# A gated mix of linear attention and a feed-forward branch: half-word stores issued from ScalarE, fewer transposing and placing transfers, later gate products, small query instructions on GpSimd, and a new order

## The chip, the cores and the metric

The kernel runs on one core of one Trainium2 chip. The metric is the device time of one execution in microseconds (us). The profiled execution is a single one; the times are given as the median of the runs.

## The reference

For x of 2048 rows and 640 columns, 32 heads of 20 columns, and a feed-forward width of 1728, cut to what matters:

```python
qkv = (x @ wqkv).reshape(B, S, 3, H, Dh)            # H = 32, Dh = 20
pq, pk = q . w_phi, k . w_phi                       # per head, 20 x 20
phi = concat([softmax(p), softmax(-p)])             # 40 features per head
kv, z = phi_k^T v, sum_s phi_k                      # per head
o = (phi_q kv) / (phi_q z + 1e-6)
a = o @ wo                                          # branch A
b = silu(x @ w1) @ w2                               # branch B
g = sigmoid((x * gate_w).sum(-1))                   # one number per row
return g * a + (1 - g) * b
```

## The kernel before, in words

All matrix products run in fp32 with each operand split into a high and a low half and three passes (`PASSES`), so a "split" (`split`, line 228) is a copy on ScalarE and a subtraction on VectorE or GpSimd. The kernel has three stages. First the k and v projections of all rows and their features, and most of branch B. Then a tail (`TAIL`): the last tiles of branch B, the fused query weights, the split of `wo`, the query tiles t = 12 to 15, the gating of branch B's output (`out_store`, line 1267: product with 1 - g on GpSimd, then a store of the block to `fb_d` in DRAM), and the first splits of x (`xb`, line 228). Then the final stage (`FIN`): query tiles b = 0 to 11 (rows 0 to 1535), and for every pair of tiles, called a unit u, the rest of branch A. Units 0 and 1 are the tiles 12 to 15 of the tail; a unit has 256 rows.

A query tile goes: projection pq on TensorE (line 594, 30 matmuls), subtractions of maxima on VectorE, exponential on ScalarE, a product with z on GpSimd (`q_norm`, `ez`, line 1343), a sum on VectorE, small instructions on 128x32 and 128x64 (`q_parts`, `q_inv`, `q_weights`: lines 1354 to 1373), the weighting on GpSimd (`q_mul`, `eq`, line 1379), and two copies on ScalarE that write each fp32 number as two 16-bit half-words (`q_out`, lines 1389 and 1393). Two stores bring the half-words to DRAM (`m_d` and, for the last 128 columns, `t_d`). Transposing DMAs bring a unit's features back with features on partitions (`q_in`, `fT`, lines 1407 and 1411). Then pn (`n_mm`, line 1734) multiplies them with kv, and pr (`r_mm`, line 1758) the remainder that does not fill a group. The results become `oT`, split by `n_hi` and `n_lo`; those of pr are split into `rT`, stored to `r_d` (line 1771) and placed into spare partitions of `oT` by further transfers (`r_place`, line 1779). pa (`w_mm`, line 1811) multiplies oT with wo, for one or two units per oT; `w_add` adds branch B's block, loaded from `fb_d` into `y` (line 1803), and stores the result (line 1823).

`TAIL` and `FIN` are strings of names in which every name is one step. They fix the order of the instructions on TensorE, VectorE, ScalarE and GpSimd. The names used below: in `FIN`, `q{b}p`, `m`, `s`, `e`, `z`, `S`, `P`, `i`, `k`, `M`, `g` are the parts of a query tile in the order above, `j{u}{k}` transposes, `n{u}{i}` is pn, `z{u}m` is pr, `z{u}d` places, `w{p}{m}` is pa, `d{p}{m}` adds, `x..l` and `x..s` load and split a part of x. SP, which issues the DMAs, gets its order from a scheduler that follows the other engines. The DMAs share eight semaphores in turn, so an issue waits until the transfer that used its semaphore before has ended. The buffer `raw` has four slots, `oT` two.

Of the kernel before, what the change touches and what calls it, by code (L numbers as in the profile page):

```python
# [8 lines left out]
F32 = mybir.dt.float32  # L9
# [8 lines left out]
P = 128  # L18
S = 2048
D = 640  # L20
# [56 lines left out]
hm012 fm0 fs0 fl2 fl3 wa fl5 fm5 fs5 xl2 fm2 hp012 fl1 fs2 fl4 fm1 fs1 fm3 fs3 xs2 fm4 xl1 fs4 hm013  # L77
hp013 qp13 q013 wb q113 im0 km xs1 qe13 qs13 qc13 qp12 q012 qn13 q112 qe12 qN13 qP13 qs12 qc12 qn12
ia0 im1 qp14 q014 W qi13 ol1 qN12 ia1 q114 qw13 ol4 qm13 qP12 qi12 qw12 qm12 os1 hm112 qp15 q015 kp
hm113 ol0 qg13 qe14 qn14 qg12 q115 qs14 qe15 qc14 im2 qN14 ig3 qs15 hp112 qn15 ia2 qc15 qP14 qi14  # L80
ol3 qw14 qm14 hp113 im3 ia3 im4 qN15 ia4 im5 qP15 qi15 ig1 os3 ia5 im6 ia6 ig0 qw15 qm15 ol2 xl0 os2
j0 im7 qg14 ig6 ig7 os0 j1 ia7 im8 ia8 im9 j2 xs0 ig5 qg15 os4 ig8 ig9 ia9 ig2 ig4
# [61 lines left out]
TPOSE = (NP - 1,)  # L144
FIN = """
x8l q0p q0m q0s0 x3s z0m n00 n01 x6l j10 q0s1 q1p x5l z0h z0l h00 q0e q0z l00 q0S q1m q1s0 q1s1 n04
x8s x10l n10 j12 q0Z x4s n02 n11 n03 x11l h02 z1m l02 n14 j11 q0P q1e h01 n12 x7l z1h q1z n13 h10
l01 q0i x5s q2p z1l x11s q0k q1S z0d q1Z q1P h12 h11 l12 q1i q1k q0M l10 q1M x10s l11 q0g q3p q2m
q2s1 q1g z1d w00a w00b x7s q2s0 x9l q2e q2z q3m q3s1 w02a w02b q3s0 d00 q2S q3e q2Z x6s q3z q2P q2i
q2k q2M w03a q2g q3S q3Z q3P q3i q3k q3M q3g q4p q4m q4s0 q5p j20 j21 d02 j32 q4s1 q4e q4z j22 q5m  # L150
w04a z2m q5s1 w04b q5s0 z2h q5e q4S z2l n20 n21 d04 w01a q4Z q4P h20 q4i q4k q5z w01b x16l q5S x9s
q5Z q4M d01 q7p n22 n23 q4g h21 q5P l20 q7m x14l x12l n24 j30 q5i h22 z3m j31 w03b z3h n32 z3l q7s1
q5k l22 q7s0 l21 n33 x16s h31 n30 n31 h30 n34 h32 l31 l30 l32 q7e q5M q7S q6p q7z x12s z2d d03 z3d
q5g j40 w10a j42 x14s x13l q6m q6s0 q6s1 w10b w14a q7Z q7P w14b q7i q7k x13s q6e q6z q6S q8p q6Z q7M
q9p q7g z4m q6P n44 n40 q6i q6k q6M q6g q8m q8s0 d14 d10 q8s1 q8e q9m q8z n41 x17l j50 q9s0 q9s1 z4h
z4l q9e q8S x15l h40 w12a q8Z j41 w12b q8P q8i q8k h42 q9S j52 l40 q9z d12 w11a x15s w11b d11 j51
x17s q11p n42 n43 h41 q9Z q9P l42 n52 n53 q11m h51 n54 h52 q9i n50 l41 q8M q9k q9M n51 l52 z5m l51
z5h q10p w13a z5l z4d q8g h50 l50 q9g j62 q10m q10s1 q10s0 w13b z5d j61 w20a d13 q11s1 w23a w21a
w23b q10e w22a q11s0 q10S q10z w22b q10Z q11e q10P w21b w20b j60 q11S n60 n61 q10i n64 q11z q11Z h60
h62 n62 n63 q11P q11i z6m h61 z6h q10k q10M q11k q11M d22 t73 f73 t74 f74 d21 t71 f71 t72 t70 d20  # L160
t75 w24a f75 f72 w24b z7m n74 d23 l62 n72 f70 l60 n73 z6l l61 d24 z7h n70 n71 z6d w32a h70 w32b w34a
w34b z7l w30a w30b l70 h71 l71 d32 h72 l72 z7d w42a d34 w40a w42b w40b d30 d42 d40 w44a w44b d44
# [8 lines left out]
def mix_kernel(ctx: ExitStack, tc: tile.TileContext, xT, wqT, wkc, wkr, wv, bd, bdc, wo, w1, w1r, w2, out):  # L171
# [101 lines left out]
    m_d = [dp.tile([256, 2, 2 * D], U16, name=f"m_d{u}") for u in range(NP)]  # L273
    t_d = [dp.tile([256, 2, P], U16, name=f"t_d{u}") for u in range(NP)]
    r_d = [dp.tile([2, REST, 256], F32, name=f"r_d{u}") for u in range(NP)]
# [990 lines left out]
    def out_store(h, j, m):  # L1266
        nc.gpsimd.tensor_tensor(acc[j][m], acc[j][m], gates[j], op=ALU.mult)  # L1267
# [21 lines left out]
    def q_proj(t):  # L1289
# [3 lines left out]
        else:  # L1293
# [3 lines left out]
            sums[t] = pq[:, 0, HALF : HALF + 2 * H]  # L1297
# [34 lines left out]
    def q_scale(t):  # L1332

        if t // 4 == NB - 1:
            sm = Q[t]["sm"]
            nc.scalar.activation(sm[:, 6 * H :], sums[t], AF.Copy, scale=g[:, t : t + 1])
            nc.scalar.activation(sm[:, 4 * H : 5 * H], halves(sums[t])[:, :, 0], AF.Copy, scale=1e-6)
# [10 lines left out]
    def q_parts(t):  # L1348

        s, sm = sums[t], Q[t]["sm"]  # L1350
        w, parts = sm[:, 2 * H : 4 * H], halves(sm[:, 4 * H : 6 * H])
        first, other = halves(w)[:, :, 0], halves(s)[:, :, ::-1]
        if t // 4 == NB - 1:
            nc.gpsimd.tensor_tensor(first, sm[:, 4 * H : 5 * H], first, op=ALU.add)
            nc.gpsimd.tensor_tensor(parts, halves(w), other, op=ALU.mult)
        else:
            nc.vector.scalar_tensor_tensor(first, halves(s)[:, :, 0], 1e-6, first, op0=ALU.mult, op1=ALU.add)
            nc.vector.tensor_tensor(parts, halves(w), other, op=ALU.mult)
# [7 lines left out]
    def q_weights(t):  # L1366
# [3 lines left out]
        if t // 4 == NB - 1:  # L1370
            nc.gpsimd.tensor_tensor(halves(w), halves(sm[:, 6 * H :])[:, :, ::-1], rb, op=ALU.mult)
        else:
            nc.vector.scalar_tensor_tensor(  # L1373
# [562 lines left out]
```

## Time and profile before

| What | Value |
|---|---|
| median of 3 runs | 717.36 us (714.91 to 717.88) |
| the profiled execution's own time | 714.72 us |
| its span | 712.9 us |
| mean granted TensorE clock | 0.993 |
| instructions | 11989 |
| HBM traffic | 87.56 MB read, 48.02 MB written |

The profile gives each engine's busy time, the waits of an engine grouped by what ended them, the timeline of an engine (start, busy time, tile, count, and in brackets the idle time before), and windows with the granted clock. PE is TensorE's matmul part, DVE VectorE, ACT ScalarE, POOL GpSimd, SP the engine that issues DMAs here ("SPq" is its issuing). A wait is put down to what came last. The tail's query tiles start near 480 us; the final stage starts near 543 us.

### The profile page before, as it was taken

The page shows a single profiled execution, that of the slowest core. Times are in us where ns is not written, and L with a number is a line of the kernel's source. Part 1 is how long each engine was busy: PE and PEld are TensorE (multiplying, and loading weights), DVE is VectorE, ACT ScalarE, POOL GpSimd, SP SyncE. Part 2 cuts the span into 40 slices and gives each one's busy share as a digit, 9 for nine tenths or more (in the row PEclk, how much of TensorE's full clock was granted, in tenths as well). Part 3 has the DMA queues.
Part 4 walks back from the last instruction along what each step waited for, and adds up shares of the span by engine and source line. Part 5 has one row for each costly group of instructions (what it writes and reads, how often), then busy time and mean ns, then how long its engine had stood idle before and what let it go on. Part 6 is the DMA issues. An engine that isn't in the chain of part 4 may idle for free.

```text
span 712.9 us, 11989 instructions
## 1 busy us (share of the span) xinstructions
PE 692.9 (97%) x4492; PEld 585.5 (82%) x4492; DVE 469.4 (66%) x774; ACT 310.1 (43%) x544; POOL 389.2 (55%) x296
## 2 busy tenths in 40 slices
PE   8999999999999999999999999999999789899997
PEld 7888888888888888888888888778987668688877
DVE  4587988886343556678525656666886869868832
ACT  5444454546555243235344324435383344633330
POOL 2367876585743465132875547801579776646320
PEclk9999999999999999999999999999999999999999
DMA  8458878676775557185966633473077776788753
GB/s 305 139 180 300 320 269 319 241 279 229 228 250 168 186 207 243 52 294 199 302 223 228 216 109 114 171 216 99 19 196 235 199 201 191 229 191 196 213 158 100
DMA packets 98968, 146.46 MB, mean 205 GB/s; under 512 B 47779, under 2 KB 63159, under 8 KB 98911
## 3 DMA queue, kind: packets, MB, share of 16 engines
q1 hardware_dynamic: 98910, 145.71, 63.6%
q8 instruction: 35, 0.57, 0.3%
q14 instruction: 23, 0.18, 0.1%
HBM read 87.56 MB, written 48.02 MB: 190 GB/s over the span
## 4 chain that ended last, share of the span: by engine, by line
PE 82%; DMA 7%; DVE 3%; POOL 2%; SPq 2%; ACT 2%; issue 2%; POOLq 0%; DVEq 0%
PE kvp L618 17%; PE o L1234 11%; PE a L1104 9%; PE pa L1811 8%; PE o L1193 8%; PE pq L594 5%; PE b L1104 3%; PE c L1104 3%; PE d L1104 3%; PE o_m L1256 3%; DMA oT<-r_d 2%; PE ph L684 2%; PE hp L703 2%; PE kvt L605 1%; DMA out<-y 1%
## 5 line engine op out<-in xcount | busy, mean ns | idle before, releaser
L1224 DVE TENSOR_TENSOR acc<-acc,o 128x512 f32<-128x512 f32 x104 | 68.4, 683 | 35.3 <-PE o L1234 35.2
L618 PE MATMUL kvp<-wh,xa 128*128 128x480 f32 (+2 forms) x420 | 90.3, 358 | 0.0
L1811 PE MATMUL pa<-oT,wo 128*128 128x512 f32 (+1 forms) x375 | 75.0, 359 | 6.8 <-DMA oT<-r_d 4.2
L1193 PE MATMUL o<-u,w 128*128 128x512 f32 x340 | 81.2, 390 | 0.1
L618 PEld LDWEIGHTS kvp<-wh,xa 128*128 128x128 f32 x420 | 72.8, 188 | 9.9
L1811 PEld LDWEIGHTS pa<-oT,wo 128*128 128x128 f32 x375 | 61.3, 194 | 18.8 <-issue 8.6
L1193 PEld LDWEIGHTS o<-u,w 128*128 128x128 f32 x340 | 63.5, 188 | 14.0 <-DVE u L677 0.5
L1343 POOL TENSOR_TENSOR ez<-eq,zbc 128x1280 f32<-128x1280 f32 x16 | 47.2, 2953 | 27.6 <-ACT eq L1326 25.9
L594 PE MATMUL pq<-wq,xb 128*128 128x320 f32 x360 | 55.2, 311 | 1.4 <-POOL xb L228 1.4
L594 PEld LDWEIGHTS pq<-wq,xb 128*128 128x128 f32 x360 | 53.1, 188 | 4.1 <-issue 1.8
L1120 POOL TENSOR_TENSOR u<-v,u 128x512 fp32r<-128x512 f32 x16 | 20.7, 1292 | 64.2 <-ACT u L1119 64.2
L1118 ACT ACTIVATE v<-v 128x512 f32<-128x512 f32 x33 | 20.9, 632 | 78.8 <-DVE v L1137 36.5
L646 POOL TENSOR_TENSOR ek<-ek,st 128x1280 f32<-128x1280 f32 x16 | 38.3, 2394 | 30.9 <-DVE st L645 25.7
L1088 POOL TENSOR_TENSOR v<-v,v 128x512 f32<-128x512 f32 x32 | 41.6, 1302 | 13.7 <-DVE u L1120 7.0
L618 PE MATMUL kvp<-wl,xa 128*128 128x480 f32 (+2 forms) x210 | 47.6, 356 | 0.0
L1379 POOL TENSOR_TENSOR eq<-eq,sm 128x1280 f32<-128x1280 f32 x16 | 38.3, 2397 | 14.2 <-DVE sm L1373 13.8
L1389 ACT COPY ez<-eq 128x2400 uint16<-128x2400 uint16 x14 | 30.7, 2194 | 31.3 <-POOL eq L1379 31.3
L228 POOL TENSOR_TENSOR xb<-xrb,xb 128x512 fp32r<-128x512 f32 (+1 forms) x18 | 19.6, 1098 | 41.8 <-PE pwq L346 26.1
L228 POOL TENSOR_TENSOR xa<-xra,xa 128x512 fp32r<-128x512 f32 (+1 forms) x26 | 28.4, 1112 | 23.8 <-ACT xa L226 17.6
L618 PEld LDWEIGHTS kvp<-wl,xa 128*128 128x128 f32 x210 | 36.6, 188 | 4.8
L1120 DVE TENSOR_TENSOR u<-v,u 128x512 fp32r<-128x512 f32 x25 | 19.9, 797 | 29.5 <-ACT u L1119 28.1
L1267 POOL TENSOR_TENSOR acc<-acc,G 128x512 f32<-128x512 f32 x20 | 28.7, 1458 | 13.7 <-DVE acc L1198 13.7
(251 smaller groups left out, 1542.2 us busy)
## 6 DMA issues: line engine op xcount, KB each, us to landing
w<-w_d SPq DMA_DIRECT2D x20, 640.0 KB
w_d<-aw SPq DMA_DIRECT2D x14, 640.0 KB
m_d<-ez SPq DMA_DIRECT2D x14, 640.0 KB
sa<-s_d SPq DMA_DIRECT2D x16, 512.0 KB
xr<-xT SPq DMA_DIRECT2D x27, 256.0 KB
ra<-w SPq DMA_DIRECT2D x18, 320.0 KB
wb<-w_d SPq DMA_DIRECT2D x9, 640.0 KB
w_k<-w SPq DMA_DIRECT2D x8, 640.0 KB
```

The costliest lines, as they stand in the source:

```text
L228: eng.tensor_tensor(lo, src, hi.bitcast(F32), op=ALU.subtract)
L594: nc.tensor.matmul(dst, xt[c][:, hx, :], w[:, c, hw, lo : lo + n], start=first, stop=(hx == 1 and c == NC - 1))
L618: nc.tensor.matmul(kv_cols(t, lo, hi), xt[c][:, hx, :], WKV[hw][:, c, w_cols(lo, hi)], start=(n == 0), stop=(n == 3 * NC - 1), skip_group_ ...
L646: return lambda: nc.gpsimd.tensor_tensor(groups(e), groups(e), spread(st[:, 1, :]), op=ALU.mult)
L1088: nc.gpsimd.tensor_tensor(v[i], v[a], v[b], op=ALU.subtract)
L1104: last["mm"] = nc.tensor.matmul(out, lhs, rhs, start=(first and i == 0), stop=(stop and i == len(todo) - 1), skip_group_check=True)
L1120: eng.tensor_tensor(u[:, 1, :], v, u[:, 0, :].bitcast(F32), op=ALU.subtract)
L1193: nc.tensor.matmul(o, lhs, rhs, start=(n == 0), stop=(n == len(todo) - 1))
L1224: nc.vector.tensor_tensor(acc[j][m], acc[j][m], o, op=ALU.add)
L1234: nc.tensor.matmul(o, ws[hw], x()[hx], start=(first and i == 0), stop=(i == len(PASSES) - 1), skip_group_check=True)
L1343: nc.gpsimd.tensor_tensor(ez, Q[t]["e"], zbc, op=ALU.mult)
L1811: nc.tensor.matmul(pa[:, a, :], wo_tile[0][:, c, hw, ds], o[:, ho, c, :size], start=(i == 0), stop=(i == len(TERMS) - 1),)
```

## The change

Five edits, and with them new strings for `TAIL` and `FIN`.

1. In `q_out` the two stores of half-words are issued by ScalarE, not SP. The 128 last columns go into `m_d` beside the others, so `t_d` is gone, and `q_in` needs three transposing DMAs for a unit, not four.
2. `r_d` and `oT` are laid out so that `r_place` needs two transfers for a unit, not four.
3. The small steps `q_parts` and `q_weights` of the twelve tiles of `FIN` run on GpSimd (three instructions) with two scalings on ScalarE (`q_scale`), as those of tiles 12 to 15 already do, not on VectorE.
4. The low half of the split of `wo` (five times 128x640) is computed on GpSimd.
5. The gate products of block 2 of branch B (rows 1024 to 1535) leave the tail: they are done in `FIN` on the loaded block `y` (`w_gate`, names `c{p}{m}`), with a load of the gates of its own (`late_gates`, name `gl`) into one of the four raw slots.

```diff
 TAIL = """
-hm012 fm0 fs0 fl2 fl3 wa fl5 fm5 fs5 xl2 fm2 hp012 fl1 fs2 fl4 fm1 fs1 fm3 fs3 xs2 fm4 xl1 fs4 hm013
+hm012 hp012 ol2 fl5 ol3 fl4 fm0 ol4 xl1 fl2 fl3 fm5 fs5 fm4 fm3 fl1 fm1 fs0 fm2 fs4 fs3 km fs2 xs1
...
 FIN = """
-x8l q0p q0m q0s0 x3s z0m n00 n01 x6l j10 q0s1 q1p x5l z0h z0l h00 q0e q0z l00 q0S q1m q1s0 q1s1 n04
+q0p j12 x4s x5l q1p z0m n00 q0m q0s1 q0s0 q1m q0e q0z n01 q1s0 q1s1 x3s x5s n02 q1e j11 x6l q0S q0c
...
     def out_store(h, j, m):
-        nc.gpsimd.tensor_tensor(acc[j][m], acc[j][m], gates[j], op=ALU.mult)
         b = 2 * h + j
+        if b != NB - 2:
+            nc.gpsimd.tensor_tensor(acc[j][m], acc[j][m], gates[j], op=ALU.mult)
...
-        split(wo_tile[0][:, c, 0], wo_tile[0][:, c, 1], r[:, :D])
+        split(wo_tile[0][:, c, 0], wo_tile[0][:, c, 1], r[:, :D], "pool")
...
     def q_scale(t):
 
-        if t // 4 == NB - 1:
-            sm = Q[t]["sm"]
-            nc.scalar.activation(sm[:, 6 * H :], sums[t], AF.Copy, scale=g[:, t : t + 1])
-            nc.scalar.activation(sm[:, 4 * H : 5 * H], halves(sums[t])[:, :, 0], AF.Copy, scale=1e-6)
+        sm = Q[t]["sm"]
+        nc.scalar.activation(sm[:, 6 * H :], sums[t], AF.Copy, scale=g[:, t : t + 1])
+        nc.scalar.activation(sm[:, 4 * H : 5 * H], halves(sums[t])[:, :, 0], AF.Copy, scale=1e-6)
...
-            nc.vector.scalar_tensor_tensor(first, halves(s)[:, :, 0], 1e-6, first, op0=ALU.mult, op1=ALU.add)
-            nc.vector.tensor_tensor(parts, halves(w), other, op=ALU.mult)
+        nc.gpsimd.tensor_tensor(first, sm[:, 4 * H : 5 * H], first, op=ALU.add)
+        nc.gpsimd.tensor_tensor(parts, halves(w), other, op=ALU.mult)
...
+        nc.gpsimd.tensor_tensor(halves(w), halves(sm[:, 6 * H :])[:, :, ::-1], rb, op=ALU.mult)
...
-        nc.sync.dma_start(m_d[u][rows], main)
-        nc.sync.dma_start(t_d[u][rows], rest)
+        nc.scalar.dma_start(m_d[u][rows, :, : 2 * D], main)
+        nc.scalar.dma_start(m_d[u][rows, :, 2 * D :], rest)
...
-        n = min(4, 2 * NG - 4 * k)
+        n = min(4, 2 * NG + 1 - 4 * k)
...
         if n < 4:
-            nc.sync.dma_start_transpose(d[:, n], t_d[u].rearrange("t s c -> (t s) c"))
-            fTs[u, NG] = f[:, n * 256 : (n + 1) * 256]
+            fTs[u, NG] = f[:, (n - 1) * 256 : n * 256]
...
     def r_place(u):
         for side in range(2):
             rows = slice(side * CT + KD, (side + 1) * CT)
-            for s in range(2):
-                nc.sync.dma_start(
-                    o_cols(u)[rows, s].bitcast(F32),
-                    r_d[u][s, side * REST // 2 : (side + 1) * REST // 2].rearrange("(c r) s -> r c s", r=CT - KD),
-                )
+            nc.sync.dma_start(
+                o_cols(u)[rows].rearrange("r c s w -> r (c s) w").bitcast(F32),
+                r_d[u][side * REST // 2 : (side + 1) * REST // 2].rearrange("(r c) s w -> r (c s) w", r=CT - KD),
+            )
...
+    def w_gate(p, m0):
+        y = ws[p, m0][0]
+        n, size, at = w_parts(p, m0)
+        at -= (NB - 2) * 512
+        g = gates["late"][:, None, at : at + size].to_broadcast([P, n, size])
+        nc.gpsimd.tensor_tensor(y, y, g, op=ALU.mult)
```

The order moves at three places that matter below. On TensorE, where the tail meets the final stage, before (pq_5481 is the second query tile of `FIN`, q1, pq_5592 the third, q2; two more pq follow it, and then the first pa):

```order
L594 MATMUL pq_5481<-wq,xb_4_4893 128x320
L1734 MATMUL pn_2_5533<-fT_2_5393,kvw 64x256 x2
L1734 MATMUL pn_0_5541<-fT_0_5478,kvw 64x256 x2
L1758 MATMUL pr_5561<-fT_2_5544,kvwr 64x128 x2
L1734 MATMUL pn_2_5565<-fT_2_5544,kvw 64x256 x2
L1734 MATMUL pn_1_5574<-fT_1_5568,kvw 64x256 x4
L594 MATMUL pq_5592<-wq,xb_0_5465 128x320 x2
```

And now, with pq_5521 for q2 and pq_5626 for q3:

```order
L1730 MATMUL pn_0_5488<-fT_0_5395,kvw 64x256 x4
L595 MATMUL pq_5521<-wq,xb_0_5504 128x320 x2
L1730 MATMUL pn_1_5566<-fT_1_5514,kvw 64x256 x4
L1763 MATMUL pr_5574<-fT_2_5444,kvwr 64x128 x2
L1730 MATMUL pn_2_5577<-fT_2_5303,kvw 64x256 x2
L1730 MATMUL pn_0_5621<-fT_0_5619,kvw 64x256 x2
L595 MATMUL pq_5626<-wq,xb_0_5504 128x320 x2
```

Unit 1's pr and most of its pn now come behind q2's projection; behind them q3, q4 and q5 stand ahead of the first pa, where q2 and q3 stood. On GpSimd the end of the tail and the start of `FIN`, before:

```order
L1379 TENSOR_TENSOR eq_5189<-eq_5189,sm_5187 128x1280
L1267 TENSOR_TENSOR acc_3_2400<-acc_3_2400,G_2_5113 128x512
L228 TENSOR_TENSOR xb_0_5396<-xrb_0_5337,xb_0_5396 128x512
L1267 TENSOR_TENSOR acc_1_2406<-acc_1_2406,G_3_5115 128x512
L228 TENSOR_TENSOR xb_0_5465<-xrb_0_5422,xb_0_5465 128x512
L1343 TENSOR_TENSOR ez_5525<-eq_5461,zbc 128x1280
L228 TENSOR_TENSOR xb_4_5536<-xrb_4_5426,xb_4_5536 128x256
```

And now:

```order
L1370 TENSOR_TENSOR eq_5208<-eq_5208,sm_5206 128x1280
L1270 TENSOR_TENSOR acc_1_2398<-acc_1_2398,G_3_4983 128x512
L230 TENSOR_TENSOR xb_2_5446<-xrb_2_5408,xb_2_5446 128x512
L1343 TENSOR_TENSOR ez_5498<-eq_5443,zbc 128x1280
L230 TENSOR_TENSOR xb_0_5504<-xrb_0_5406,xb_0_5504 128x512
L230 TENSOR_TENSOR xb_4_5507<-xrb_4_5449,xb_4_5507 128x256
L1353 TENSOR_TENSOR sm_5441<-sm_5441 128x32
```

The products with G_2 are gone, both xb splits of the second pair of tiles stand behind the products with G_3, one of them behind the first tile's ez, and the small instructions follow. On SP around the placing transfers of unit 1 (into oT_5522), before:

```order
L1779 DMA oT_5522<-r_d_119 4x5x256 x2
L1394 DMA m_d_104<-ez_5525 128x2560
L1395 DMA t_d_112<-sm_5459 128x256
L321 DMA xrb_2_5945<-xT 128x2x256
L1394 DMA m_d_104<-ez_5581 128x2560
L1407 DMA_TRANSPOSE fT_0_5862<-m_d_104 128x4x512
```

And now (into oT_5560):

```order
L1783 DMA oT_5560<-r_d_110 4x10x256 x2
L322 DMA xrb_2_5684<-xT 128x2x256
L1783 DMA oT_5560<-r_d_111 4x10x256
L1398 DMA_TRANSPOSE fT_0_5734<-m_d_104 128x4x512
L1783 DMA oT_5560<-r_d_111 4x10x256
L1398 DMA_TRANSPOSE fT_1_5829<-m_d_104 128x4x512
L1398 DMA_TRANSPOSE fT_2_5856<-m_d_104 128x3x512
```

The stores are no longer in SP's row. Between the two placing transfers of unit 1 stands the first transpose of unit 2 (m_d_104).

More of the change, by code (lines that the diff above doesn't have):

```diff
@@ L272, in mix_kernel @@
     g_d = dp.tile([NT, P], F32, name="g_d")
-    m_d = [dp.tile([256, 2, 2 * D], U16, name=f"m_d{u}") for u in range(NP)]
-    t_d = [dp.tile([256, 2, P], U16, name=f"t_d{u}") for u in range(NP)]
-    r_d = [dp.tile([2, REST, 256], F32, name=f"r_d{u}") for u in range(NP)]
+    m_d = [dp.tile([256, 2, 2 * D + P], U16, name=f"m_d{u}") for u in range(NP)]
+    r_d = [dp.tile([REST, 2, 256], F32, name=f"r_d{u}") for u in range(NP)]
     X = {}
@@ L1707, in mix_kernel @@
             ):
+                if part is q_out and PB.index(t // 2) in TPOSE:
+                    continue
                 ops[f"{name}{t}"] = lambda t=t, part=part: part(t)
-        for k in range(3):
+        for k in range(0 if 0 in TPOSE else 3):
             ops[f"j{k}"] = lambda k=k: q_in(0, k)
@@ L1849, in mix_kernel @@
                 ops[f"d{p}{m0}"] = lambda p=p, m0=m0: w_add(p, m0)
+                if p > 2:
+                    ops[f"c{p}{m0}"] = lambda p=p, m0=m0: w_gate(p, m0)
+        ops["gl"] = late_gates
         for b, t in enumerate(QT):
```

92 lines of the change are left out of this document (51 added, 41 removed).

## The prediction

> **What bounds the kernel now.** I read the page first, then the list of waits, TensorE's timeline after 540 us, its clock by windows, and SP's and POOL's timelines around each wait. The page:
>
> ```profile
> PE 692.9 (97%) x4492; PEld 585.5 (82%) x4492; DVE 469.4 (66%) x774; ACT 310.1 (43%) x544; POOL 389.2 (55%) x296
> ```
>
> TensorE is busy 97% of the span, and the order of the two kernels shows the same matmuls in both. So only time in which TensorE waits or runs slowly can be won. All its waits after 480 us, as total, times, longest:
>
> ```profile
> PE pa L1811 <- DMA oT<-r_d: 4.2, 4, 3.4
> PE pr L1758 <- DMA fT<-t_d: 3.8, 1, 3.8
> PE pa L1811 <- DMA out<-y: 2.7, 1, 2.7
> PE pq L594 <- POOL xb L228: 1.4, 1, 1.4
> PE pwq L346 <- DMA wTq<-wqT: 1.2, 1, 1.2
> PE pn L1734 <- DVE sm L1363: 0.7, 1, 0.7
> ```
>
> They add up to 14.0 us. The timeline shows that more is lost behind three of them (start, busy time, count, wait in brackets):
>
> ```profile
> 546.03 3.19 PE L594 MATMUL pq<-wq,xb 128*128 128x320 f32 x20 [1.40 <-POOL xb L228]
> ...
> 561.12 0.69 PE L1758 MATMUL pr<-fT,kvwr 128*64 128x128 f32 x4 [3.76 <-DMA fT<-t_d]
> 561.57 2.80 PE L1734 MATMUL pn<-fT,kvw 120*64 120x256 f32 x12
> 564.30 9.28 PE L594 MATMUL pq<-wq,xb 128*128 128x320 f32 x60
> 577.02 10.54 PE L1811 MATMUL pa<-oT,wo 128*128 128x512 f32 x38 [3.44 <-DMA oT<-r_d]
> ...
> 622.56 8.67 PE L1811 MATMUL pa<-oT,wo 128*128 128x512 f32 x30 [2.65 <-DMA out<-y]
> ...
> 641.62 7.16 PE L1811 MATMUL pa<-oT,wo 128*128 128x512 f32 x30
> ...
> 654.93 2.38 PE L1734 MATMUL pn<-fT,kvw 120*64 120x256 f32 x20 [0.75 <-DVE sm L1363]
> ```
>
> The undisturbed price of 30 pa is 7.16 us, and the same 30 took 8.67 behind the wait of 2.65: 1.51 too many. 38 pa should take 38/30 x 7.16 = 9.07 and took 10.54: 1.47. Twelve pn should take 12/20 x 2.38 = 1.43 and took 2.80: 1.37. The windows say why; the last number but two of each row is the granted clock:
>
> ```profile
> 561.00:564.30 3.30, 3.18 (x16) 1.80 (x16) 2.50 (x5) 1.06 (x3) 2.17 (x2) 0.50 0.77 176
> 577.00:587.50 10.50, 10.48 (x39) 8.33 (x40) 5.00 (x9) 1.75 (x3) 7.42 (x5) 0.84 0.91 241
> 622.50:631.20 8.70, 8.64 (x31) 7.01 (x32) 7.28 (x14) 2.36 (x2) 6.24 (x4) 0.81 0.91 218
> 641.60:648.70 7.10, 7.10 (x33) 5.82 (x32) 6.93 (x12) 2.84 (x5) 6.85 (x4) 1.00 0.92 230
> ```
>
> Each of the three waits is followed by a stretch at a lowered clock, which costs about 1.45 us more (4.35 in all); the wait of 1.40 us is not (20 pq in 3.19 us is the rate of the 60 in 9.28). The pool to win from is 14.0 + 4.35 = 18.4 us. The Trainium skill ("TensorE: Matmul & The Clock Gate", section "Part 1: The HAM clock gate") says that the clock falls to half after about 3.4 us of idleness and needs 3.4 us of work to come back; the 0.50 behind 3.76 us agrees, while 2.65 us, which by it should have cost nothing, did lower the clock here. By the page the third stretch could not be won back by shortening its wait, and the sum below would be 1.5 us worse.
>
> **What ends these waits.** SP issues all transfers in one row, so what stands ahead there delays what TensorE needs (issue time, then the tile):
>
> ```profile
> 558.23 1.25 SPq L1411 DMA_TRANSPOSE fT<-t_d  x1
> ...
> 570.09 0.59 SPq L1779 DMA_DIRECT2D oT<-r_d  x2
> 572.70 0.37 SPq L1394 DMA_DIRECT2D m_d<-ez  x1
> ...
> 573.59 1.27 SPq L1779 DMA_DIRECT2D oT<-r_d  x2
> ```
>
> The fourth transpose of unit 1 leaves at 558.23, and pr of that unit waits for it until 561.12. The last two placing transfers stood behind a store that had to wait for ScalarE's copies: all of SP's waits of this kind, and the landing (from the chain) of the transfer that pa waits for:
>
> ```profile
> SPq L1394 <- ACT sm L1393: 13.4, 7, 3.8
> 573.59 3.30 DMA oT<-r_d
> 609.63 5.52 DMA out<-y
> 616.83 2.97 SPq L1779 DMA_DIRECT2D oT<-r_d  x8
> ```
>
> At the second oT the output store of 609.63 was under way for 5.52 us; SP's next issue after the stores behind it stood until 615.1, and the eight placing transfers left from 616.83 on.
>
> **The change part by part.**
>
> Stores on ScalarE. 28 issues leave SP, and with them SP's 13.4 us of waiting for the copies. ScalarE waits only for its own copies, so no wait for them is new; but an issue can stand until the transfer that had its semaphore before has ended. Bounds for 28 issues: 0.37 us each (row at 572.70), 10 us of an engine that is busy 43%, so nothing on the path; at worst a block of 3.8 us (the longest above) once or twice, behind which stand the splits of xb and the oT copies. I take 0.5 us on the path.
>
> Fewer transfers. The fourth transpose (1.25 us of SP) goes in seven units, and the remainder comes with the last transpose. Placing takes 2 instead of 4 per unit; each costs about 0.3 to 0.37 us (0.59 for 2, 2.97 for 8), 16 fewer is 5 to 6 us of SP over 150 us. These bring forward by 1.2 and 0.6 us what stands behind; alone that shortens the waits of 3.76 and 3.44 by as much.
>
> The order of TensorE. A whole pair of query tiles' worth of work moves: pq2 now stands ahead of pr and most of pn of unit 1, pq4 and pq5 stand ahead of the first pa, pq8 and pq9 ahead of the second oT's pa. One pq is 30 matmuls, half of 9.28: 4.6 us. So pr of unit 1 has 4.6 us more cover, plus 1.2, against a wait of 3.76; the first pa 9.3 more against 3.44; the second oT's pa 9.3 more against 2.65. If transfers kept their times, all three would vanish, with their slow stretches.
>
> They don't keep them: the cover moves the next unit's stores and transposes too. In SP's new order the last placing transfer of unit 1 stands behind the first transpose of unit 2, which waits for unit 2's stores. I follow that unit through POOL with the rows of the next part, in the times of before. xb for pq2 is complete at 555.7 (worked out there); then come a split of 0.73, an ez of 2.95, two mul of 2.40, the small ops of two tiles (1.8) and ScalarE's copies, for which 2.6 is taken (mul's length and a little): 568.6. POOL's waits for its partners are 3.0 us a tile now (24.1 + 13.9 less 1.7, over 12), so one to two tiles' waits make it 571.6 to 574.6; I take 573.1. The store lands some 1.5 later, the transpose takes 1.25 to issue as at 558.23, and the placing transfer behind it 0.6 and 3.30 as above: 579.8. pa stood at 577.0; without the earlier waits and their slow stretch (1.4 + 0.6 + 3.76 + 1.37 + 3.44 = 10.6), with two pq more ahead (8.9, the two in 9.28 less their modelled end) and the new waits below (2.0 + 0.3) it is due at 577.6. So 2.2 us of wait and one slow stretch of 1.45 stay (between 0.7 with none and 5.2 with it, for the 1.5 us either way). The pa of the second oT comes out even (its transfers land 0.2 us before it is due): 0 to 5, I take 1.0.
>
> POOL. Its rows (all after 540 us, by form; busy, mean | idle before):
>
> ```profile
> L1343 POOL TENSOR_TENSOR ez<-eq,zbc 128x1280 f32<-128x1280 f32 x12 | 35.3, 2948 | 24.1 <-ACT eq L1326 22.4 <-DMA m_d<-ez 1.7
> L1379 POOL TENSOR_TENSOR eq<-eq,sm 128x1280 f32<-128x1280 f32 x13 | 31.2, 2403 | 13.9 <-DVE sm L1373 13.8
> L228 POOL TENSOR_TENSOR xb<-xrb,xb 128x512 fp32r<-128x512 f32 x11 | 14.1, 1280 | 6.6 <-ACT xb L226 6.6
> L228 POOL TENSOR_TENSOR xb<-xrb,xb 128x256 fp32r<-128x256 f32 x5 | 3.6, 728 | 4.2 <-ACT xb L226 4.2
> L1267 POOL TENSOR_TENSOR acc<-acc,G 128x512 f32<-128x512 f32 x7 | 9.4, 1370 | 0.0
> L1357 DVE SCALAR_TENSOR_TENSOR sm<-pq,sm 128x32 f32<-128x32 f32 x12 | 2.3, 190 | 0.3
> L1358 DVE TENSOR_TENSOR sm<-sm,pq 128x64 f32<-128x64 f32 x12 | 2.6, 221 | 0.4
> L1373 DVE SCALAR_TENSOR_TENSOR sm<-pq,g,sm 128x64 f32<-128x64 f32 x12 | 3.2, 274 | 0.2
> L1354 POOL TENSOR_TENSOR sm<-sm x4: 253/254/256, 509.1 to 534.6; 128x32 f32<-128x32 f32 x4
> L1355 POOL TENSOR_TENSOR sm<-sm x4: 320/323/325, 509.4 to 535.0; 128x64 f32<-128x64 f32 x4
> L1371 POOL TENSOR_TENSOR sm<-sm x4: 305/500/972, 513.2 to 538.4; 128x64 f32<-128x64 f32 x4
> L1336 ACT ACTIVATE sm<-sm,g x4: 329/348/350, 503.1 to 527.0; 128x64 f32<-128x64 f32 x4
> ```
>
> The small instructions cost VectorE 190 + 221 + 274 = 0.69 us a tile, and POOL 0.254 + 0.323 + 0.305 to 0.97 = 0.88 to 1.55 us (from the four tiles that already go that way), with 0.35 and a smaller one on ScalarE. A pair of tiles holds POOL now for 2 x (2.95 + 2.40) + 2 x 1.28 + 0.73 = 14.0 us, then for 15.8 to 17.1. TensorE needs for a pair 9.28 (pq) + 2.38 (pn) + 1.25 x 7.16 (37.5 pa) = 20.6. So POOL stays under TensorE, and the handshakes sit in its idle time; but the path from pq to the store grows by 0.2 to 0.9 us a tile, which I have counted above. VectorE's 8.2 us were beside matmuls already: nothing. Here a rule speaks against the change: the Trainium skill ("GPSIMD Engine Reference", section "4.1 Engine selection") puts elementwise work on VectorE and calls GpSimd about twice as slow with two inputs; 323 against 221 ns is 1.5. By twice, a pair would hold POOL for 16.7 us.
>
> The split of wo goes to POOL five times; 128x640 lies between the 1.28 for 512 and 1.28 + 0.73 for 768 columns: 1.6 us each, 8.0 in all, against five gate products taken away, 6.9. Ahead of the tail's last mul stand the 8.0 more and three products (4.1) less:
>
> ```profile
> 539.41 2.83 POOL L1379 TENSOR_TENSOR eq<-eq,sm 128x1280 f32<-128x1280 f32 x1
> ```
>
> It ended at 542.2 and now ends up to 3.9 us later; since POOL is 55% busy, most of the five splits fall into idle time, and I take 1.1: 543.3. Then come five products (6.85), a split of xb (1.28), an ez that stood behind it before (2.95), and the other split (1.28): xb for pq2 is complete at 555.7. TensorE, rid of the first two waits but for 0.6, begins pq2's products with the low halves at about 554.2 (from 546.03: less 1.4 and 0.6, then 3.1 left of pq0, 4.6 for pq1, 1.0 for pr and six pn, 1.5 for ten matmuls). That is a new wait of 1.5 us, 2.0 with half a microsecond for POOL's hand-overs on the way; the bounds are 0.4 and 4.8 (mul later by 0 or 3.9), and with a slow stretch 6. It is shorter than the waits after which the clock fell, so I add no slow stretch.
>
> The late gate products: six on POOL, four of 1.37 and two of about 0.73, 6.9 us, of which a third stands behind the last tile, where POOL is free. They stand ahead of the last additions, which come after the matmuls; cover is there, price 0 to 0.7, I take 0. The gates' load holds one of four raw buffers, so some xb load starts later: 0 to 1.4 (the xb wait above), I take 0.3. ScalarE's two further table loads lie in the tail beside matmuls: 0.
>
> **Sum.** What stays or comes: first weight wait halved 0.6, pq2 2.0, pq4 0.3 (a split between two ez), raw buffer 0.3, first pa 2.2 + 1.45, second pa 1.0, ScalarE's issues 0.5, the small waits at the end (4.2 less 3.4 at the last oT, and a little of DVE's 0.7) 0.9 = 9.3. 18.4 - 9.3 = 9.1 us less. The profiled execution took 714.7, below the median of 717.4 and just under the lowest of the three runs; on it the sum is 705.6, on the median 708.3, which I take.
>
> **Rivals.** (1) All waits go, as the cover of 4.6 to 9.3 us alone would say: 16 to 18.4 less, 699 to 701. For it: every covered wait is under 4 us. Against: the placing behind the transpose in SP's row.
> (2) The waits only move: pq2 waits 5 to 6 us for xb with a slow stretch, the first pa keeps 5.2, the second pa gets 3 plus 1.45: about 17 against 18.4, 715 to 718. For it: POOL and SP have each got a new thing ahead of what TensorE needs.
> (3) The new issuer does not do what it says. The Trainium skill ("DMA: Bandwidth & Descriptors", section "Issuing engines are not separate DMA queues") holds that issuing from a further engine saves only the sequencer's time, usually little. As a mechanism of this kernel: the transfers land no earlier, since the engines share the load that the window at 577 shows (0.91 busy). Then 3.3 us of landing becomes 5.5 as in the output store's row, the first pa keeps another 2.2 and the second too: 4.4 less gain, about 713. Against: the wait at 573.59 was for SP's turn, not for bandwidth.
> (4) Slower: GpSimd becomes the bound of the query pairs. It holds 15.8 to 17.1 us by itself; its idle time for the partner engines is now (22.4 + 13.8)/12 = 3.0 a tile, 6.0 a pair. If that doesn't shrink, and three small ops more wait for partners, a pair takes 21.8 to 23.1 against 20.6. Six pairs at 2.0 to 2.5 are 12 to 15 us lost against 9.1 won: 720 to 724. It decides from 1.5 us a pair. Against: that idle time is mostly because POOL runs ahead.
>
> **Chances.** The forecast 0.46, with its own range 704 to 713; (1) 0.13; (3) 0.10; (2) 0.19; (4) 0.12. Faster or slower by 0.5% (about what a measurement of this kernel can tell from none) means below 713.8 or above 720.9. Faster: the forecast, (1), most of (3) and a little of (2), 0.67; same: the rest of (3), most of (2), a little of (4), 0.21; slower 0.12. The range of 699 to 719 leaves out (4) and the outermost parts of (1) and (2), under 2 in 10.
>
> **What would show it.** No wait of pr for a transposing transfer, and the 12 pn behind it at full clock; a wait of pq for xb of 1 to 4 us near 556; the first pa waiting 1 to 4 us for oT; no wait over 1.5 us at the second oT; POOL under 17.5 us busy per pair. I am wrong if POOL's ez or mul stands at the end of TensorE's waits pair after pair, if ScalarE's issues block for several us ahead of xb or oT copies, or if the transposes land later than 4 us after their issue.

## The result, and the profile after

The changed kernel is slower: 723.94 us median (722.44 to 726.0) against 716.63 of the kernel before in the same comparison, a ratio of 1.011 with a 95% interval of 1.006 to 1.015. In a second comparison it was 1.011 again (1.007 to 1.015). The profiled execution has a span of 722.2 us, 9.3 more than before. First its page, then all that TensorE waited for after 470 us (total, times, longest):

```profile
PE 694.9 (96%) x4492; PEld 586.9 (81%) x4492; DVE 455.1 (63%) x733; ACT 317.9 (44%) x570; POOL 405.2 (56%) x338
```

```profile
PE pa L1815 <- DMA out<-y: 5.6, 1, 5.6
PE pn L1730 <- DVE oT L1755: 4.5, 2, 3.2
PE pa L1815 <- DMA y<-fb_d: 3.5, 1, 3.5
PE pa L1815 <- DMA xrb<-xT: 3.3, 1, 3.3
PE pa L1815 <- DMA oT<-r_d: 2.0, 2, 1.3
PE pn L1730 <- DMA fT<-m_d: 1.5, 2, 0.9
PE pq L595 <- POOL xb L230: 1.4, 1, 1.4
PE pr L1763 <- DMA fT<-m_d: 0.2, 1, 0.2
```

These are 22.0 us, where the same list gave 14.0 before. pr's wait of 3.8 has shrunk to 0.2, as forecast, and the weights' 1.2 is gone, of which the forecast had left half. In their place stand waits of pa at every oT, 14.4 us in five places, and of pn, for VectorE above all. TensorE's timeline shows where they are and the slow work behind three of them:

```profile
554.40 3.30 PE L595 MATMUL pq<-wq,xb 128*128 128x320 f32 x20 [1.44 <-POOL xb L230]
...
565.52 0.65 PE L1730 MATMUL pn<-fT,kvw 120*64 120x256 f32 x4 [3.24 <-DVE oT L1755]
566.11 6.20 PE L595 MATMUL pq<-wq,xb 128*128 128x320 f32 x30
572.24 0.65 PE L1730 MATMUL pn<-fT,kvw 120*64 120x256 f32 x4
572.82 9.06 PE L595 MATMUL pq<-wq,xb 128*128 128x320 f32 x60
585.22 8.71 PE L1815 MATMUL pa<-oT,wo 128*128 128x512 f32 x30 [3.34 <-DMA xrb<-xT]
...
632.70 7.47 PE L1815 MATMUL pa<-oT,wo 128*128 128x512 f32 x31 [3.49 <-DMA y<-fb_d]
...
671.45 17.67 PE L1815 MATMUL pa<-oT,wo 128*128 128x512 f32 x68 [5.63 <-DMA out<-y]
```

30 pq took 6.20 us where half of 9.06 is due (1.7 too many), 30 pa took 8.71 for 7.16 (1.55), and 68 pa took 17.67 for 16.23 (1.4): 4.6 us, about the 4.35 of before. So 8.0 us more of waits and 0.3 more of slow work stand against the 9.3 that the span has grown. By the two pages the 9.3 are 7.3 us of idle time and 2.0 of busy time; of the busy time the slow stretches account for 0.3, and the rest isn't traced here. In a wait for transfers the profile names whatever landed last; SP's timeline tells more. Around the first pa of the changed kernel:

```profile
577.88 0.62 SPq L1783 DMA_DIRECT2D oT<-r_d  x1
578.60 2.18 SPq L1398 DMA_TRANSPOSE fT<-m_d  x1
580.84 0.63 SPq L1783 DMA_DIRECT2D oT<-r_d  x1
```

The last placing transfer does stand behind the transpose, as forecast. But SP had stood still for 7.9 us ahead of the first of these two, and not for a store:

```profile
SPq L1783 <- DVE oT L1755: 7.9, 1, 7.9
```

The placing writes rows of oT that `n_lo` also writes, so it waits for all of the unit's low halves. These are late for two reasons. One of unit 1's products stands on TensorE behind the projection of 566.11, which itself came late and ran slow; it starts at 572.24 (above), and its copy on ScalarE ends at 573.5. And on VectorE five instructions of the next tiles, from 572.34 on, stand ahead of the two halves, which start at 576.80: about 3.3 us of the wait are VectorE's fixed order. Besides, each issue itself costs more than it did. The issues of the store to r_d and of the placing, before and then changed (minimum, median, maximum in ns):

```profile
L1771 SPq DMA_DIRECT2D r_d<-rT x16: 274/344/496, 559.6 to 690.1; - x16
L1779 SPq DMA_DIRECT2D oT<-r_d x32: 242/295/851, 562.5 to 697.3; - x32
```

```profile
L1776 SPq DMA_DIRECT2D r_d<-rT x16: 752/790/1091, 562.7 to 700.9; - x16
L1783 SPq DMA_DIRECT2D oT<-r_d x16: 612/653/1345, 567.5 to 703.9; - x16
L1385 ACTq DMA_DIRECT2D m_d<-ez x14: 541/542/644, 521.2 to 665.2; - x14
L1386 ACTq DMA_DIRECT2D m_d<-sm x14: 541/580/825, 521.9 to 665.9; - x14
```

Half as many placing transfers take the same time in all (32 x 0.295 = 9.4 us, 16 x 0.653 = 10.4), and the store to r_d, of which there are as many as before, takes 16 x 0.446 = 7.1 us more.

### The profile page after: what moved, and what is told of

It is laid out like the page before. It is cut to its first block, busy times and chain, and to the rows that moved or that the text cites. A ratio compares the mean times of both kernels' runs of the same rounds, so it can differ in the third digit from the quotient of the medians.

```text
span 722.2 us, 11976 instructions
## 1 busy us (share of the span) xinstructions
PE 694.9 (96%) x4492; PEld 586.9 (81%) x4492; DVE 455.1 (63%) x733; ACT 317.9 (44%) x570; POOL 405.2 (56%) x338
## 4 chain that ended last, share of the span: by engine, by line
PE 87%; DMA 5%; DVE 3%; SPq 2%; issue 1%; POOL 0%; ACT 0%; ACTq 0%; POOLq 0%
PE kvp L619 17%; PE o L1194 11%; PE o L1235 11%; PE a L1105 9%; PE pa L1815 8%; PE pq L595 6%; PE ph L685 3%; PE b L1105 3%; PE c L1105 3%; PE d L1105 3%; PE o_m L1257 3%; DMA out<-y 2%; PE hp L704 2%; DMA oT<-r_d 2%; PE kvt L606 1%
## 5 line engine op out<-in xcount | busy, mean ns | idle before, releaser
L230 POOL TENSOR_TENSOR xb<-xrb,xb 128x512 fp32r<-128x512 f32 (+1 forms) x18 | 19.8, 1106 | 26.6 <-ACT xb L228 25.9
L1105 PE MATMUL a<-xo,wc 128*128 128x512 f32 x132 | 33.5, 389 | 0.0
```

The source lines that it names most:

```text
L230: eng.tensor_tensor(lo, src, hi.bitcast(F32), op=ALU.subtract)
L1105: last["mm"] = nc.tensor.matmul(out, lhs, rhs, start=(first and i == 0), stop=(stop and i == len(todo) - 1), skip_group_check=True)
```

## Experiments

All ratios are to the kernel before, timed on the same chip in the same comparison. In two kernels, `order_alone` and `small_on_vector`, the VectorE form of the small steps reads the sums after the reciprocal has been written over them, so that their output isn't the reference's. The number, shape and order of their instructions are those meant, and their times are used for that alone.

**The order and the edits, apart.** First all edits in the old order; then the new order without the edits.

> All five edits of the change, but with the order of TAIL and FIN before; only the steps that did not exist before are added to it (the scalings right behind a tile's sum, the late gates' load behind unit 1's first copy of pn's result, each late product ahead of its addition). Theory 1 (the new order puts transposes and long waits ahead of the placing transfers): the edits alone win what they save on SP, 710 to 716 us, and TensorE's waits for pn behind VectorE are absent. Theory 2 (the edits themselves, above all small instructions on GpSimd and the placing that waits for the whole unit, cost the time): 720 us or more, with pn or pa waiting as in the changed kernel.

> The new order of TAIL and FIN with none of the other edits: stores on SP, four transposes and four placing transfers for a unit, the small query instructions on VectorE (on sums kept in SBUF, as the new order needs the PSUM bank free), the split of wo on VectorE, the gate products of block 2 in the tail. Theory 1 (the order is at fault): 722 us or more, since SP then has more to issue in the same places. Theory 2 (the edits are at fault): 708 to 714 us.

```diff
# parts_in_old_order: strings of before, with the new names put in
-... q0e q0z l00 q0S q1m ...
+... q0e q0z l00 q0S q0c q1m ...
# order_alone, in the changed kernel: each edit taken back
-        nc.scalar.dma_start(m_d[u][rows, :, : 2 * D], main)
+        nc.sync.dma_start(m_d[u][rows], main)
```

Measured: 734.08 us, 1.028 (1.026 to 1.031), and 728.29 us, 1.021 (1.018 to 1.023). The first is in the range of theory 2, the second in that of theory 1, so neither theory alone holds: each half alone is slower than the two together. The order needs the edits, the edits need the order, and the cost has to be looked for piece by piece.

**Two edits taken back in the changed kernel.**

> The changed kernel with the three small query instructions of the twelve late tiles back on VectorE, reading sums in SBUF; no scalings on ScalarE for them. Theory A (VectorE stands still in its fixed row for small results that are queued behind GpSimd's long products, and so releases the banks of pn late): the two waits of pn for VectorE (3.2 and 1.3 us) and the slow 1.6 us behind the first go, and the transposed units come earlier: 714 to 719 us. Rival (VectorE is late by its own work and the order): the waits stay within 1 us of these and the time within 721 to 726.

> The changed kernel with the stores of half-words issued by SP again (three transposes for a unit and the joint buffer stay). Theory A (ScalarE's issues that wait for a semaphore of another transfer hold up the oT copies): TensorE's wait of 3.5 us at the second oT goes, 717 to 721 us. Rival (SP is the crowded row, and taking the stores off it helped): 726 to 732 us, with longer waits of pa.

```diff
# small_on_vector, in q_parts and q_weights
-        nc.gpsimd.tensor_tensor(parts, halves(w), other, op=ALU.mult)
+        nc.vector.tensor_tensor(parts, halves(w), other, op=ALU.mult)
# stores_on_sp, in q_out
-        nc.scalar.dma_start(m_d[u][rows, :, 2 * D :], rest)
+        nc.sync.dma_start(m_d[u][rows, :, 2 * D :], rest)
```

Measured: the small instructions on VectorE 728.2 us, 1.019 (1.015 to 1.022). They do not help in the new order; against the changed kernel's 1.011 they cost some 5 us there. Theory A falls, and the time is above the rival's range too. The stores on SP 722.2 us, 1.011 (1.009 to 1.014): who issues the stores makes no difference to the time. pn's long wait for VectorE went, the first pa's wait grew to 7.5 us, and neither expectation was met.

**The other edits, taken back one at a time.**

> The changed kernel itself, beside the others on one chip. Both theories: 1.007 to 1.015 of the kernel before, 719 to 726 us, with a first pa that waits 3 to 4 us and slow pa behind it.

> The changed kernel with the placing of before: r_d and oT in their old layouts, four placing transfers for a unit. In the changed kernel's trace an issue of the r_d store takes 0.79 us on SP where it took 0.34 before, and one of the two placing transfers 0.65 where one of the four took 0.30: the merged layout saves no issue time and costs 16 x 0.45 = 7 us of SP. Theory D (SP's time decides when the second and third oT are whole): issue times fall back to 0.34 and 0.30, the waits of pa (3.5 and 5.6 us) shrink by 2 us or more, 717 to 721 us. Rival (SP has room, and the order decides): within 1.5 us of the changed kernel's time on this chip.

> The changed kernel with the joint buffer undone: the last 128 half-word columns go to a buffer of their own, and a unit takes four transposes. Stores took 0.54 + 0.58 us to issue in the changed kernel, 0.36 + 0.39 before. Theory D: the stores' issues fall back to these times, SP issues seven more transposes of about 1.2 us; if SP is what counts, 724 to 730 us and longer waits of pn and pr for transposes. Rival (the joint buffer's slower stores are what hurts): 717 to 721 us.

> The changed kernel with the gate products of block 2 back in the tail and no late load. Theory (the raw slot and the late products cost nothing): xb for the third tile is 4 to 7 us later, since five more products stand ahead of it on GpSimd, and pq waits that long: 724 to 730 us. Rival (the raw slot held to the end delays loads of x and with them the first pa, which the trace names as waiting for an xb load): 717 to 721 us.

```diff
# old_placing: r_d, oT, the store in r_lo and r_place as before
-        oTs[p] = tb.tile([P, NG, 2, 512], F32R, tag="oT", name=f"oT{p}", bufs=2)
+        oTs[p] = tb.tile([P, 2, NG, 512], F32R, tag="oT", name=f"oT{p}", bufs=2)
# four_transposes
+        nc.sync.dma_start_transpose(d[:, n], t_d[u].rearrange("t s c -> (t s) c"))
# gates_early, in out_store
-        if b != NB - 2:
+        if True:
```

Measured: the changed kernel 721.02 us, 1.011 (1.007 to 1.015); with the old placing 714.45 us, 1.0005 (0.998 to 1.003); with four transposes 721.21 us, 1.012 (1.008 to 1.016); with early gates 725.76 us, 1.017 (1.014 to 1.020). The old placing came out below both of its ranges. So the placing with its new layouts is what the change lost, about 1% or 7 us. The late gates gain some 5 us, as their theory had it, and the joint buffer is even. TensorE's waits with the old placing (four longest groups):

```profile
PE pn L1730 <- DVE oT L1755: 4.5, 2, 3.2
PE pa L1816 <- DMA oT<-r_d: 2.6, 1, 2.6
PE pa L1816 <- DVE sm L1360: 2.5, 1, 2.5
PE pa L1816 <- DVE eq L586: 2.3, 1, 2.3
```

The two waits at the last two oT are gone and the others of pa are shorter; pn's are not. At the end of the kernel the chain from rT to oT of the last two units can be read off SP's timeline; with the old placing, and then the changed kernel in the same comparison:

```profile
682.92 0.69 SPq L1776 DMA_DIRECT2D r_d<-rT  x2
686.51 1.30 SPq L1784 DMA_DIRECT2D oT<-r_d  x4
...
690.23 0.67 SPq L1776 DMA_DIRECT2D r_d<-rT  x2
693.17 1.28 SPq L1784 DMA_DIRECT2D oT<-r_d  x4
```

```profile
687.17 1.68 SPq L1776 DMA_DIRECT2D r_d<-rT  x2
691.86 1.36 SPq L1783 DMA_DIRECT2D oT<-r_d  x2
...
697.23 1.65 SPq L1776 DMA_DIRECT2D r_d<-rT  x2
700.35 1.36 SPq L1783 DMA_DIRECT2D oT<-r_d  x2
```

From the store's issue to the end of the placing's issues it is 4.9 and 4.2 us with the old placing, and 6.1 and 4.5 with the new: the two stores of a unit alone take 1.0 us longer to issue.

**The store or the placing.**

> The changed kernel with half of its placing undone: r_d and oT keep the new layout (so the store from rT to r_d, 0.79 us to issue), but a unit is placed by four transfers, not two. Theory D1 (the store's new form is the slow part: from its issue to the placing 4.7 us at the end of the kernel, where the old placing took 2.9): 718 to 722 us, pa still waits at the two last oT. Theory D2 (the merged placing transfers, which wait for all of a unit's halves and land later, are the slow part): 713 to 717 us.

> The changed kernel with the other half undone: r_d in its old layout with the old store (0.34 us to issue), but a unit is placed by two transfers. Theory D1: 713 to 717 us. Theory D2: 718 to 722 us.

> The kernel before, its order and all its steps, with only the new layouts of r_d and oT and two placing transfers for a unit. Theory D (the placing chain of every unit is 2.4 us longer, from the end of rT to pa): each of the four waits of pa for oT grows by up to 2.4 us, 717 to 724 us, 3 to 10 more than before. Rival (it costs only where the new order has no slack): within 2 us of before.

```diff
# merged_store_only, in r_place
+            for s in range(2):
+                nc.sync.dma_start(o_cols(u)[rows, :, s].bitcast(F32), ...)
# merged_placing_only, in r_lo
-                r_d[u][:, :, k * P : (k + 1) * P], t[k * CT : k * CT + REST].bitcast(F32)
+                r_d[u][:, :, k * P : (k + 1) * P].rearrange("s r c -> r s c"), t[k * CT : ...]
```

Measured: 724.59 us, 1.014 (1.010 to 1.017); 716.34 us, 1.003 (1.000 to 1.005); 717.74 us, 1.005 (1.002 to 1.007). Theory D1 fits better, though the first time lies above its range: with the store back in its old form, two placing transfers are nearly as good as four. The issues in the kernel with the merged placing only, then in that with the merged store only:

```profile
L1776 SPq DMA_DIRECT2D r_d<-rT x16: 289/336/660, 563.4 to 692.6; - x16
L1783 SPq DMA_DIRECT2D oT<-r_d x16: 609/630/761, 566.5 to 695.5; - x16
```

```profile
L1776 SPq DMA_DIRECT2D r_d<-rT x16: 752/788/1109, 562.2 to 697.6; - x16
L1784 SPq DMA_DIRECT2D oT<-r_d x32: 611/616/828, 566.6 to 701.9; - x32
```

The last row is a flaw of that experiment: four transfers out of the new layout cost 0.62 each, not 0.30, so it charges the store with some 9 us of SP that are the placing's. It also shows what made a placing transfer dear. In the new layout one of four costs 0.62 and one of two 0.65, so merging does halve the issue time there; but the new layout doubles the price of each. The comparison of the changed kernel with the merged placing only is clean of the flaw, and gives 1.011 against 1.003 (each in its own comparison). SP's order at the end of the kernel is the same in these two, while with the old placing the last unit's store goes ahead of a load of `y`; with the merged placing only, the chains of the last two units take 4.9 and 3.9 us against the 6.1 and 4.5 above. The issues of the store differ between these two as 0.79 and 0.34 us; whether the store also lands later was not separated from that. In the old order the new placing costs 0.5%, at the lower edge of theory D's range.

**What the order left.** With the old placing the new order is even with before, not 9 us faster. SP had the cause in its waits: 8.9 us in one piece for VectorE's halves.

> The changed kernel with the old placing, and in FIN a few steps moved: on VectorE the low half that frees a bank of pn (l02) goes ahead of the wait for GpSimd's small result, the two low halves of unit 1 ahead of the next tile's subtractions and the sum, one low half of unit 3 ahead of a sum; and the first transposes of the next unit behind the placing of units 1 and 3. TensorE's order is the same. Theory E (SP's placing stood for up to 8.9 us for halves that were late in VectorE's fixed row, and for transposes; the bank was late for the same reason): the waits of 3.2 (pn), 2.6 and 2.5 us (pa) shrink to under 1 each, with slow stretches 8 to 10 us less than with the old placing alone: 704 to 709 us. Rival (what is moved back makes new waits: the later subtractions and transposes): 712 to 717 us.

> The version with the old placing and the halves moved ahead, and besides unit 1's third transpose ahead of a load of x and of the late gates on SP. In the version without that, pn waited 3.1 us for this transpose (issued at 561.7 behind the two loads, 1.8 us) and the next tile's projection ran slow behind it. Theory E: the wait shrinks by 1.5 to 2 us and the slow stretch shortens, 707 to 710 us. Rival (the load of x that comes later holds the next projection): 711 to 714 us.

> The changed kernel, its own placing included (new layouts, store of 0.79 us, two placing transfers), with only the steps of FIN moved as in the version with the halves ahead. Theory D (the store's form lengthens the chain of every unit from rT to pa by 2.4 us; where there is slack it costs nothing): 714 to 718 us, the first pa no longer waits over 1 us, the last two oT still cost 1 to 1.5 us each. Rival (the loss was the halves' place in the order alone): 710 to 713 us.

```diff
# steps of FIN, in the changed kernel's string (excerpts)
-... x8s q1i q1k q1M j10 n10 h02 q2s1 q3p l11 q2s0 n11 l02 ...
+... x8s h02 l02 q1i q1k q1M j10 n10 q2s1 q3p l11 q2s0 n11 ...
-... q3m q0g q3s1 x6s q2e q3s0 ... h10 q2z x9s q2S l10 l12 q2c q4p j20 ...
+... q3m q0g x6s q2e ... h10 q2z x9s l10 l12 q3s1 q3s0 q2S q2c q4p ... z1d j20 ...
# transpose_earlier, besides
-... n02 q1e j11 x6l ... z1h gl x9l ... j10 n10 ...
+... n02 q1e j11 j10 x6l ... z1h x9l ... h02 gl l02 ...
```

Measured: 711.75 us, 0.995 (0.993 to 0.998); 708.37 us, 0.991 (0.988 to 0.994); with the changed kernel's own placing 721.52 us, 1.008 (1.005 to 1.010). The first came out between its two ranges (704 to 709 and 712 to 717): it gained, but less than theory E had it, since pn now waited for a transpose. The second met its theory. The third is above both of its ranges: the new layouts, with store and placing, cost over 1% where the halves are early, too. In it the first pa no longer waits, but the third oT's pa waits 5.1 us. TensorE's waits, with the halves ahead and then with the transpose ahead besides:

```profile
PE pn L1713 <- DMA fT<-m_d: 4.6, 3, 3.1
PE pa L1799 <- DMA oT<-r_d: 2.2, 1, 2.2
```

```profile
PE pa L1799 <- DMA oT<-r_d: 2.8, 1, 2.8
PE pn L1713 <- DVE oT L1738: 2.7, 3, 1.3
PE pq L578 <- DVE eq L569: 1.8, 1, 1.8
PE pq L578 <- POOL xb L213: 1.4, 1, 1.4
PE pn L1713 <- DMA fT<-m_d: 0.9, 1, 0.9
PE pr L1746 <- DMA fT<-m_d: 0.7, 2, 0.4
```

pa waits at one oT only, in both. The last version has 10.3 us of waits and is the fastest measured, 6 to 7 us under the kernel before.

**Why the edits cost so much in the old order.**

> The kernel before and its order, with only the three small query instructions of the twelve late tiles on GpSimd, and the two scalings on ScalarE. Theory F (in an order made without them, each hand-over makes VectorE and GpSimd stand for the other in their fixed rows): 720 to 728 us, 1 to 2 % slower, with waits of pq and pn behind them. Rival (GpSimd has room, the hand-overs sit in its idle time, as forecast): 712 to 716 us.

> The kernel before with its own order and placing and the small instructions on VectorE, and with the other edits: stores on ScalarE, joint buffer with three transposes, split of wo on GpSimd, late gates. Theory F: without the small instructions on GpSimd and the new store of rT these edits cost little or win: 709 to 718 us against the 734 of all edits in the old order. Rival: 722 us or more.

```diff
# small_on_gpsimd_in_before: the kernel before, with q_parts, q_weights and q_scale of the changed one
-            nc.vector.scalar_tensor_tensor(first, halves(s)[:, :, 0], 1e-6, first, op0=ALU.mult, op1=ALU.add)
+        nc.gpsimd.tensor_tensor(first, sm[:, 4 * H : 5 * H], first, op=ALU.add)
# other_edits_in_old_order: parts_in_old_order without these and with the old placing
```

Measured: 725.95 us, 1.015 (1.012 to 1.018), and 713.99 us, 0.999 (0.996 to 1.002). Both met theory F. The small instructions alone, with the sums that they need kept in `sm` instead of in pq's bank, cost the old order 10 to 11 us. VectorE's waits in that kernel say how:

```profile
DVE sm L1330 <- POOL ez L1327: 14.4, 8, 6.9
DVE sm L1343 <- POOL sm L1338: 13.2, 8, 4.0
```

and the one of these two that the kernel before has:

```profile
DVE sm L1346 <- POOL ez L1343: 1.1, 2, 0.6
```

VectorE stands 27.6 us for GpSimd where it stood 1.1, and all that is behind it in its row stands with it. In the changed kernel, whose order was laid out with them, the second of these waits is 4.8 us and the first isn't among those listed. Of the 2.8% that all edits cost in the old order, the small instructions (1.5) and the new placing (0.5) explain 2.0; the rest isn't traced.

## Why the prediction was wrong

The forecast was 708.3 us, 9.1 less than before, in a range of 699 to 719; the changed kernel took 723.94. On the profiled executions 9.1 us less were forecast and 9.3 more came. By the terms of the sum, what stays or comes was put at 9.3 us and is 26.6 (22.0 of waits and 4.6 of slow work). The excess lies at the second and third pa (9.6 us more than forecast), in pn's waits with the slow work behind them (7.7), and at the first pa and the last two oT (1.2 and 1.1); the other terms came out some 2 us lower.

- The pool was read rightly: waits of 14.0 us and 4.35 us of slow work. pr's wait went from 3.8 to 0.2 us, the weights' from 1.2 to nothing.
- The step that failed is the pricing of "Fewer transfers". It said of a placing transfer "each costs about 0.3 to 0.37 us" and halved their number; in the new layout a merged one takes 0.65, and even one of four takes 0.62. And the store to r_d, whose layout the same edit changes, was not priced at all: it went from 0.34 to 0.79 us, sixteen times, and twice in every chain from rT to pa. Instead of 5 to 6 us less, SP got 8 us more from these two (7.1 + 1.0). Undoing it brought 1.011 to 1.0005, the whole loss.
- The second term that failed is the second and third pa, 1.0 and 0 forecast, 3.5 and 5.6 measured. With the old placing they are 2.5 and 2.3, and with the halves ahead only the third is left, at 2.2. So with the placing undone the new order still gave none of the 9.1 us; it gave 0.5% when the halves came earlier, and 0.9% with one transpose and two loads exchanged.
- The third is pn, put at nothing beyond "a little of DVE's 0.7". Its wait of 3.24 us for VectorE, with 1.7 us of slow work behind it, was not foreseen. The bank of pn that it needed was freed by a low half (565.03) behind a hand-over with GpSimd and two subtractions. In the changed kernel's other profiled execution pn waited at the same place 2.1 us for a transpose, so removing one wait uncovers the other.
- The first pa: 2.2 and 1.45 us forecast, 3.34 and 1.55 measured. The number is near, but its cause was only half right: the transpose was ahead, but the unit's stores, forecast for 573.1, had left ScalarE by 571.2, and SP had waited for VectorE's halves, which the working never followed. The working also took 1.5 us from a store's issue to its landing; in the kernel before a transpose stood until 599.26 for a store issued at 596.24, 3.0 us. It decided nothing here.
- pq's wait for xb: forecast 2.0, measured 1.44, with xb split at 554.4 where the working had 555.7; GpSimd's part of the working held. That no slow stretch followed was luck in part. The working argued that the wait was shorter than those after which the clock fell, but a wait of 1.82 us in the last version with the transpose ahead was followed by a granted clock of 0.72.
- The joint buffer's stores were priced at 0.37 us too and took 0.54 to 0.58; that cost nothing that could be measured (1.012 with it undone). ScalarE as issuer was rightly put near nothing: 1.011 either way. There rival 3's rule came out right: who issues made no difference.
- Rival 4 named the hand-overs between VectorE and GpSimd as the slower case, 720 to 724 us. The measured time lies in that range, but by luck: in the old order the hand-overs do cost 1.5%, in the new order taking them out costs more. So they aren't what made the change slower.
- The late gates were put at nothing and the wait for xb at 2.0; undone, the wait for xb was 3.9 and the time 4 to 5 us more. That term held.

What stays open: why the store to r_d takes 0.79 us to issue in one layout and 0.34 in the other, though both move the same bytes, and the changed kernel and the one with only its store put back have the same count of packets, 102263. Open, too, is why a placing transfer of the same 20 KB costs 0.62 us in one layout and 0.30 in the other. Undoing the placing (7 us), moving the halves (4) and moving the transpose (3) together account, by a rough count over three comparisons, for about 14 of the 18 us between forecast and measurement; the rest isn't traced.

## What to carry to other kernels

Fewer transfers are less issue time only if a transfer keeps its price: here the layout that allowed the merging doubled it. Price the new access pattern by a row of its own shape, and price every transfer whose layout the merge changes, those at the other end of the buffer too. A placing transfer here waited for every writer of the rows that it touches (7.9 us for VectorE's halves), so before a queue's order is blamed, look at what its longest wait is for. Moving work between engines with fixed orders is a change of the order: the same instructions cost 1.5% in one order and were needed in another, so an edit that is timed alone in the old order can tell the wrong sign.

## What the runs showed of the hardware that was not expected

In these runs the time of an issue on SP or ScalarE follows the layout, not the engine. The two stores of a tile's half-words took 0.34 to 0.39 us where a row is one run of bytes, and 0.54 to 0.60 where it is two, on either engine.

And the length of a wait doesn't tell whether the clock drops. After the wait of 3.49 us in the changed kernel it didn't, after 3.24 and 3.34 it did (the last number but two is the granted clock):

```profile
565.50:572.00 6.50, 6.48 (x34) 6.12 (x34) 0.00 (x0) 5.08 (x6) 5.86 (x4) 0.74 0.84 222
585.20:594.00 8.80, 8.78 (x32) 6.86 (x34) 6.83 (x10) 4.59 (x5) 7.72 (x8) 0.81 0.76 204
632.70:640.10 7.40, 7.40 (x31) 5.75 (x32) 2.67 (x4) 4.30 (x4) 3.19 (x3) 1.00 1.13 277
```

In the other profiled execution of the same kernel the two waits of pa have changed places. The 30 pa behind the first ran undisturbed (granted clock 1.00), the 31 behind the second took 1.5 us too many (0.81):

```profile
585.68 7.13 PE L1815 MATMUL pa<-oT,wo 128*128 128x512 f32 x30 [3.35 <-DMA xrb<-xT]
...
631.69 8.91 PE L1815 MATMUL pa<-oT,wo 128*128 128x512 f32 x31 [3.58 <-DMA y<-fb_d]
```

So a slow stretch of 1.5 us behind a wait can come and go between two executions of one kernel. With the 2.65 us in the kernel before and the 1.82 us above, which were followed by a lowered clock, this fits a window that runs free of the wait's start, as the Trainium skill says ("TensorE: Matmul & The Clock Gate", section "Part 1: The HAM clock gate"). Its length of 3.4 us is not borne out: an idle window of that length could miss a wait of 3.49 us, but waits of 1.82 or 2.65 us could not fill one.
